# Eight views for the scattered results, and token tiles prepared only six places ahead, in a planned FFT and mixture-of-experts kernel

## The chip, the cores and the metric

The kernel runs on one core of one Trainium2 chip. The metric is the device time of one execution in microseconds (us). The engines carry the profile's names: PE (TensorE, matrix products), DVE (VectorE), ACT (ScalarE), POOL (GpSimd) and SP (SyncE, which here only starts DMAs).

## The reference

An input of 8 batches of 2496 rows by 256 columns goes through a real FFT along the rows, a complex 256x256 product with a bias, a soft threshold on real and imaginary part, and the inverse FFT. The 19968 rows that come out are tokens of a mixture of 8 experts, one expert for each token:

```python
Yr = Xr @ w_r - Xi @ w_i + b_r          # X = rfft(x, axis=1)
Yi = Xr @ w_i + Xi @ w_r + b_i
...                                      # soft threshold at 0.01
y = irfft(Y, n=2496)                     # 19968 tokens of 256
e_idx = argmax(y @ w_gate)               # one expert for each token
for e in range(8):
    h = maximum(y[mask] @ w1[e], 0.0)    # 256 -> 1024
    ye = h @ w2[e]                       # 1024 -> 256
    out[mask] = gate_w * eom * ye        # two factors for each token
```

Every product runs as three f16 products of values split into a high and a low half, so a matrix has two f16 parts.

## The kernel before, in words

The first part computes the FFT stages for one batch after another and writes the tokens `y`, with the two factors and the routing, to a DRAM tensor `yd`. The second part works on tiles of 128 tokens of one expert: T_A = 64 tiles in phase A, made of the tokens of batches 0 to 3 and taken in blocks of two tiles while the later batches still go through the FFT, and then 99 tiles in phase B, one to a block (tiles 64 to 162), made of the tokens of batches 4 to 7. Tiles of one expert follow one another, so the expert changes a few times in each phase.

A tile t takes these steps:

- `gathers`: an indirect DMA on POOL's queue fetches its 128 tokens into a place `yg` (6 places).
- `tokens`: DVE takes the largest magnitude of each token (`absmax` into `ym`) and makes a power of two from it (`pow2` gives `ys`, the scale, and its inverse, which goes into `fac` with the token's two factors). ACT writes the high f16 half of the scaled tokens to `yhl` (5 places), DVE the low half. A DMA with transpose, issued by SP, brings them to `eT`. There are three `eT` buffers, each for two tiles; in phase B a tile has one half of a buffer, and an even tile shares it with the next odd one. Its place is free when the up product of the tile six before is done.
- `up`: the product with `w1` in two halves, each of 4 groups of 128 hidden values. ACT evacuates the high half of the rectified result to `hh` and DVE the low half.
- `down`: the product of `hh` with `w2`. ACT scales the result by `fac` into `o` (5 places), and an indirect DMA on POOL's queue scatters its rows to `out`.

The weights of an expert are two halves of 1 MB (part 0 for up, part 1 for down) in three buffers `wbuf0` to `wbuf2`, which the blocks use by turns; `fetch` issues a load of each half for each block on SP, under a condition: only where the expert is another than that of the block three before. A new expert therefore loads its 2 MB into each of three blocks in a row. Part 0 waits for the up product of the block three before, part 1 for its down product.

The order on each engine is written by a planner (`Issue`, `io`): each step is a generator that yields either a condition ("up" of a tile, a free place) or an engine's letter (P, A, D, G, S for PE, ACT, DVE, POOL, SP) with a due time and a duration. The planner plays these and writes one fixed order for each engine, which the engines then follow with semaphores. In `tokens` the first condition is a free `yhl` place and a free number of `fac`; the two are also what limits how far ahead a tile is prepared. `small(1, "ym", bufs=3)` takes one of three small tiles by turns.

Names of matrix products in the profile: `ps<-eT,wbuf` (L1449) is up, `ps<-wbuf,hh` (L1415) is down. L1459 and L1460 are the evacuations of up, L1431 that of down, L1434 the scatter, L1324 the gather, L1343 and L1344 the two halves of `yhl`, L1310 a weight load, L1357 a transpose. In the changed kernel these lines stand 9 further down (L1324 and L1310: 3).

Of the kernel before, what the change touches and what calls it, by code (L numbers as in the profile page):

```python
# [11 lines left out]

# [1 line left out]
F32 = mybir.dt.float32  # L14
# [10 lines left out]
N = B * S  # L25
# [10 lines left out]
T_A = -((-(NA * S - E * 255)) // 256) * 2  # L36
# [110 lines left out]
EARLY = dict(yg=3, yhl=2, eT=1, hh=1, o=1)  # L147
PLACES = dict(yg=6, yhl=5, eT=3, hh=2, o=5)
UP, DN = 2.8, 1.4
KW = 4  # L150
YR, ZR, AN, WR, SR = 2, 3, 6, 3, 6
S1 = 6
# [35 lines left out]
class Issue:  # L188
# [64 lines left out]
    def give(self, slots, n=1):  # L253
        for _ in range(n):
            if slots.queue:
                self.go(slots.queue.pop(0))
            else:
                slots.n += 1
# [25 lines left out]
def tile_fft_moe(ctx, tc, x, w_r, w_i, b_r, b_i, w_gate, w_og, w1, w2, f1, f4, cmat, gmat, m16, out, dbg=None):  # L284
    nc = tc.nc
    V, A, G, T = nc.vector, nc.scalar, nc.gpsimd, nc.tensor

    pc = ctx.enter_context(tc.tile_pool(name="const", bufs=1, side="left"))
    psm = ctx.enter_context(tc.tile_pool(name="small", bufs=1, side="left"))
# [11 lines left out]
    def ring(pool, shape, dt, name, n):  # L301

        i = turn[name] = turn.get(name, -1) + 1
        return pool.tile(shape, dt, tag=f"{name}{i % n}", name=f"{name}{i % n}")

    def bank(i):
        return pps.tile([128, 512], F32, tag=f"ps{i}", name=f"ps{i}")

    def small(n, name, dt=F32, pool=psm, **kw):
        if "bufs" in kw or pool is psm:  # L310
            return ring(pool, [128, n], dt, name, kw.get("bufs", 2))
        return pool.tile([128, n], dt, tag=name, name=name)
# [71 lines left out]
    def absmax(m, src):  # L384
        V.tensor_reduce(m, src, AX.X, ALU.max, apply_absolute_value=True)

    def pow2(m, top, name, pool=psm, **kw):

        c = small(1, "p2c", bufs=3)
        V.tensor_scalar(c, m, 2.0 ** -40, 2.0 ** 60, ALU.max, ALU.min)  # L390
        e = small(1, "p2e", I32, bufs=3)
        V.tensor_scalar(e, c.bitcast(I32), 0x7F800000, None, ALU.bitwise_and)
        s = small(1, name, pool=pool, **kw)
        V.tensor_scalar(s.bitcast(I32), e, -1.0, float((254 + top) << 23), ALU.mult, ALU.add)
        inv = small(1, name + "i", pool=pool, **kw)
        V.tensor_scalar(inv.bitcast(I32), e, 1.0, float(-(top << 23)), ALU.mult, ALU.add)
        return s, inv
# [57 lines left out]
    def move(r, nbytes, issue, fn):  # L455

        yield "S", r, max(issue, nbytes / RATE), fn
# [602 lines left out]
    def plan(ph):  # L1060
# [30 lines left out]
        if ph == 0:  # L1091
            route["fl"] = pc.tile([1, T_ALL], I32, name="flg")
            route["ei"] = pc.tile([1, T_ALL], I32, name="ebi")
            V.memset(route["fl"][:, 0:2 * KW + 1], 1)
        V.tensor_copy(route["ei"][:, t0:t0 + n], ev[0:1])
        fl = lambda a, b, c, d, step: V.tensor_tensor(route["fl"][:, a:b], eb[0:1, a:b], eb[0:1, c:d:step], ALU.not_equal)
        if ph == 0:
            fl(4, 2 * KW, 0, 2 * KW - 4, 1)
            fl(2 * KW + 1, T_A, 2 * KW - 5, T_A - 6, 1)
        else:  # L1100
# [44 lines left out]
    sidx = pc.tile([128, T_ALL], I32, name="sidx")  # L1145
# [115 lines left out]


    W = []

    def open_w():
        yield "s1", B - 1
        yield "weights"
        s_x.close()
        pools["w"] = s_w.enter_context(tc.tile_pool(name="wexp", bufs=1, side="right", reuse_waits="tile"))
        for i in range(2):  # L1270
            W.append(pools["w"].tile([128, 8192], F16, name=f"wbuf{i}"))
        io.set("w open")

    def open_h():
# [3 lines left out]
        pools["h"] = s_h.enter_context(tc.tile_pool(name="hexp", bufs=1, side="left", reuse_waits="tile"))  # L1278
        W.append(pools["h"].tile([128, 8192], F16, name="wbuf2"))
        io.set("opened")  # L1280
# [4 lines left out]
    def place(k, i, shape, dt):  # L1285
        return pools["w" if i < EARLY[k] else "h"].tile(shape, dt, tag=f"{k}{i}", name=f"{k}{i}")

    def wplace(k):
        return k % 2 if k < KW else (k - KW + 2) % 3

    def before(k):

        return None if k < 2 or k == KW else k - 2 if k < KW else k - 3

    def fetch(r):

        yield "w open"
        for k, (t, n) in enumerate(BLOCKS):
            yield "plan", 0 if t < T_A else 1
            if k == KW:  # L1300
                yield "opened"
            for m in range(2):
                if before(k) is not None:
                    yield ("up", "down")[m], BLOCKS[before(k)][0]
                def f():
# [3 lines left out]
                    part = slice(4096 * m, 4096 * (m + 1))  # L1309
                    nc.sync.dma_start(W[wplace(k)][:, part], wd[ds(f, 1), :, part].rearrange("a p f -> (a p) f"), cond=g, cond_hint=False)  # L1310

# [4 lines left out]
    def gathers(r):  # L1316
        yield "w open"
        for t in range(T_ALL):
# [5 lines left out]
            yield "G", r + 5.6 * t - 30, 1.0, lambda: G.indirect_dma_start(out=yg, out_offset=None, in_=src, in_offset=bass.IndirectOffsetOnAxis(ap=gidx[:, t:t + 1], axis=0))  # L1324
            io.go(tokens(t, i, yg, r + 5.6 * t), io.now + 2.6)

    def tokens(t, iy, yg, r):

        il = yield slots["yhl"]
        yield slots["fac"]  # L1330
        m = small(1, "ym", bufs=3)
        fac = small(1, "fac", bufs=18)
        yhl = place("yhl", il, [128, 2, 256], F16)
        yield "D", r - 10, 0.41, lambda: absmax(m, yg[:, :256])

        def f():
            s, si = pow2(m, 2, "ys", bufs=3)
            V.scalar_tensor_tensor(fac, yg[:, 256:257], si, route["is"][:, t:t + 1], ALU.mult, ALU.mult)
            st["ys", t] = s

        yield "D", r - 10, 0.83, f
        s = st["ys", t]
        yield "A", r - 10, 0.5, lambda: A.activation(yhl[:, 0], yg[:, :256], AF.Copy, scale=s)  # L1343
        yield "D", r - 10, 0.48, lambda: V.scalar_tensor_tensor(yhl[:, 1], yg[:, :256], s, yhl[:, 0], ALU.mult, ALU.subtract)  # L1344
        io.put(slots["yg"], iy)
        if t >= T_A:
            ie = yield slots["eT1"]
            st["eT", t] = ie, part("eT", ie[0], [128, 2, 2, 2, 128])[:, ie[1]:ie[1] + 1]
        elif t % 2 == 0:
            ie = yield slots["eT"]  # L1350
            st["eT", t] = ie, part("eT", ie, [128, 2, 2, 2, 128])
            io.set("eT place", t)
        else:
            yield "eT place", t - 1
            st["eT", t] = st["eT", t - 1]
        eT = st["eT", t][1][:, t % 2 if t < T_A else 0]
        yield from move(r - 10, 1.4e5, 1.2, lambda: nc.sync.dma_start(eT.rearrange("p v c n -> p (v c) n"), yhl.rearrange("p v d -> p (v d)"), transpose=True))  # L1357
        st["fac", t] = fac
        yield TAIL
        io.put(slots["yhl"], il)  # L1360
        io.set("eT", t)
# [3 lines left out]
    def part(k, i, shape):  # L1365

        if (k, i) not in parts_:
            parts_[k, i] = place(k, i, shape, F16)
        return parts_[k, i]

    def back(k, t, i):

        if t >= T_A:
            io.put(slots[k + "1"], i)
            return
        st["n" + k] = st.get("n" + k, 0) + 1
        if st["n" + k] <= T_A // 2 - PLACES[k]:
            io.put(slots[k], i)
        else:
            for h in range(2):  # L1380
                io.put(slots[k + "1"], (i, h))

    def block(k, r):
# [12 lines left out]
        hh = hh.rearrange("p (v f n) -> p v f n", v=2, f=8)  # L1396
        w = W[wplace(k)][:, :4096].rearrange("p (c h v f) -> p c h v f", c=2, h=2, v=2)
        st["nu", t] = 0
        for half in range(2 * m):
            io.go(up(t, m, half, w, eT, ie, hh, r + UP * half * (m - 1)))  # L1400
        w = W[wplace(k)][:, 4096:].rearrange("p (i v c d) -> p i v c d", i=4, v=2, c=2)
        for i in range(m):
            io.go(down(t + i, m, i, w, hh, ih, r + (11.2 + 2 * UP * i + DN if m > 1 else 4)))

    def down(t, m, n, w, hh, ih, r):

        t0 = t - n
        yield "w", t0, 1

        def f(i=None):  # L1410
            if i is not None:
                st["pt", t] = i, bank(i)
            for fc in range(8 // m * half, 8 // m * (half + 1)):
                for k, (v, vw) in enumerate(((0, 0), (0, 1), (1, 0))):
                    T.matmul(st["pt", t][1][:, :256], hh[:, v, fc, 128 * n:128 * n + 128], w[:, fc // 2, vw, fc % 2], start=(fc == k == 0), stop=(fc == 7 and k == 2))  # L1415

        for half in range(m):
            for i in range(2 * half, 2 * half + 2):
                yield "hh", t0, i
            if half == 0:  # L1420
                yield "P", r, 2.62 / m, f, True
            else:
                yield "P", r + UP, 2.62 / m, f
        i, pt = st.pop(("pt", t))
        if n == m - 1:
            back("hh", t0, ih)
            io.set("down", t0)
        io_ = yield slots["o"]
        o = place("o", io_, [128, 256], F32)
        fac = st.pop(("fac", t))  # L1430
        yield "A", r - DN, 0.47, lambda: A.activation(o, pt[:, :256], AF.Copy, scale=fac)  # L1431
        io.free(i)
        give("fac")
        yield "G", r - DN, 1.0, lambda: G.indirect_dma_start(out=out, out_offset=bass.IndirectOffsetOnAxis(ap=sidx[:, t:t + 1], axis=0), in_=o, in_offset=None, bounds_check=N - 1, oob_is_err=False)  # L1434
        yield 3.6
        io.put(slots["o"], io_)

# [79 lines left out]
```

## Time and profile before

| what | value |
|---|---|
| runs | 1453.3, 1458.66, 1461.68 us (median 1458.66) |
| profiled execution | 1467.5 us, of which the span is 1465.7 |
| mean granted clock of PE | 0.991 |
| PE busy | 1410.3 us, 96% of the span |
| DVE, ACT, POOL busy | 975.2, 730.5, 646.1 us |
| phase B | about 930 to 1460 us of the span |
| HBM read and written | 337.44 and 58.91 MB |

A group of the profile names line, engine, operation and tiles (result <- operands, without buffer numbers). A time in square brackets behind an instruction is the idle time of its engine before it, with what ended it. The windows give for a stretch of the span each engine's busy time, the share of TensorE's full clock that was granted, and the busy share of the DMA engines.

### The profile page before, as it was taken

Reading aid. Unit: us, or ns where it says so; the run is one execution under the profiler, and the core shown is the slowest. Engines: PE = TensorE matmul, PEld = TensorE weight load, DVE = VectorE, ACT = ScalarE, POOL = GpSimd, SP = SyncE. Lnnn points to the kernel's source line nnn. Section 1 sums busy time; section 2 is a strip of 40 time slices with the busy share of each in tenths; the row PEclk is TensorE's granted clock in tenths of the full one; section 3 lists DMA queues with packets and bytes.
Section 4 is the critical chain, followed back from the end, with each engine's and each line's share of the span. In section 5 each row is a group of like instructions: output and inputs, shape, how many; then the busy total and the mean of one; then the engine's idle time right before and its main releaser. Section 6 shows DMA issues by size and latency. Waiting matters only on the chain.

```text
span 1465.7 us, 42645 instructions
## 1 busy us (share of the span) xinstructions
PE 1410.3 (96%) x16436; PEld 1276.6 (87%) x16436; DVE 975.2 (67%) x2789; ACT 730.5 (50%) x1413; POOL 646.1 (44%) x736
## 2 busy tenths in 40 slices
PE   5999999999999989999999999999998999999998
PEld 4998888898888868889988888899898989999898
DVE  4887767889998987787777855445454544554532
ACT  4777676868677664443333343333333333433432
POOL 2274565446575753355556343333333333433311
PEclk8999999999999999999999999999999999999999
DMA  7779899999997879976676679383846558387320
GB/s 199 174 170 212 204 233 203 229 226 224 221 218 190 180 246 178 282 210 217 192 213 209 189 234 266 100 241 92 225 125 185 166 151 237 83 239 215 97 49 24
DMA packets 294004, 276.47 MB, mean 189 GB/s; under 512 B 241846, under 2 KB 250168, under 8 KB 282025
## 3 DMA queue, kind: packets, MB, share of 16 engines
q1 hardware_dynamic: 277239, 229.68, 61.3%
q0 software_dynamic: 15872, 42.83, 10.6%
q8 instruction: 129, 2.11, 0.6%
q10 hardware_dynamic: 690, 1.24, 0.3%
q14 instruction: 74, 0.61, 0.1%
HBM read 337.44 MB, written 58.91 MB: 270 GB/s over the span
## 4 chain that ended last, share of the span: by engine, by line
PE 43%; DMA 10%; issue 4%; ACT 1%; DVE 1%; POOL 0%; POOLq 0%; SPq 0%; ACTq 0%
PE ps L1415 22%; PE ps L1449 21%; DMA eT<-yhl 4%; DMA out<-o,sidx 4%; DMA wbuf<-wd 2%; PE ps L1251 1%; ACT hh L1459 0%; DVE hh L1460 0%; ACT yhl L1343 0%; ACT o L1431 0%; DVE yhl L1344 0%; POOL out L1434 0%; POOL yg L1324 0%; POOL ob L1243 0%; POOLq L1513 0%
## 5 line engine op out<-in xcount | busy, mean ns | idle before, releaser
L1449 PE MATMUL ps<-eT,wbuf 128*128 128x128 f16 (+1 forms) x6288 | 462.4, 232 | 9.8 <-DMA wbuf<-wd 6.1
L1415 PE MATMUL ps<-wbuf,hh 128*128 128x256 f16 x3912 | 457.4, 273 | 9.2 <-ACT hh L1459 3.2
L1449 PEld LDWEIGHTS <-wbuf 128*128 128x128 f16 x6288 | 419.5, 98 | 32.6 <-DMA wbuf<-wd 7.4
L1415 PEld LDWEIGHTS <-hh 128*128 128x128 f16 x3912 | 378.4, 98 | 58.0 <-ACT hh L1459 5.1
L1460 DVE SCALAR_TENSOR_TENSOR hh<-ps,hh 128x512 f16<-128x512 f32 x326 | 219.6, 688 | 240.8 <-ACT hh L1459 215.2
L1434 POOL DMA_INDIRECT out<-o,sidx x163 | 163.2, 1001 | 427.1 <-ACT o L1431 214.6
L1459 ACT ACTIVATE hh<-ps 128x512 f16<-128x512 f32 x326 | 188.9, 596 | 270.9 <-PE ps L1449 235.0
L729 PE MATMUL ps<-whl,xt 128*128 128x256 f16 x1920 | 223.2, 273 | 0.9 <-ACT xt L714 0.7
L729 PEld LDWEIGHTS <-xt 128*128 128x128 f16 x1920 | 187.7, 98 | 32.6 <-issue 1.1
L1324 POOL DMA_INDIRECT yg<-yd,gidx x163 | 163.1, 1001 | 119.3 <-DVE yhl L1344 45.4
L1344 DVE SCALAR_TENSOR_TENSOR yhl<-yg,ys,yhl 128x256 f16<-128x256 f32 x163 | 79.0, 486 | 117.0 <-ACT yhl L1343 105.3
L1431 ACT ACTIVATE o<-ps,fac 128x256 f32<-128x256 f32 x163 | 76.9, 472 | 159.4 <-PE ps L1415 148.1
L1343 ACT ACTIVATE yhl<-yg,ys 128x256 f16<-128x256 f32 x163 | 81.9, 503 | 135.4 <-DMA eT<-yhl 83.2
L621 PEld LDWEIGHTS ps<-f1t,x 117*128 117x128 f32 (+1 forms) x704 | 88.4, 203 | 16.9 <-issue 14.6
L621 PE MATMUL ps<-f1t,x 117*128 117x120 f32 (+1 forms) x704 | 91.8, 288 | 0.2 <-ACT ste L776 0.2
L749 POOL TENSOR_TENSOR zhl<-z,zhl 128x512 f16<-128x512 f32 x54 | 62.8, 1163 | 51.0 <-ACT zhl L747 48.5
L1026 POOL TENSOR_TENSOR wsp<-wr,wsp 128x512 f16<-128x512 f32 x62 | 74.6, 1203 | 5.2
L759 PE MATMUL ps<-gt,zhl 128*128 128x128 f16 x960 | 65.5, 220 | 7.2 <-ACT zhl L747 3.0
L759 PEld LDWEIGHTS <-zhl 128*128 128x128 f16 x960 | 58.5, 98 | 14.1 <-ACT zhl L747 3.2
L825 PE MATMUL ps<-bdt,f4t 120*117 120x512 f16 x264 | 70.5, 382 | 0.1
L630 ACT ACTIVATE at<-ps,sx 128x480 f16<-128x480 f32 (+1 forms) x88 | 55.8, 650 | 28.8 <-PE ps L621 26.3
L631 DVE SCALAR_TENSOR_TENSOR at<-ps,sx,at 128x480 f16<-128x480 f32 (+1 forms) x88 | 59.2, 695 | 12.4 <-ACT at L630 12.1
(195 smaller groups left out, 1652.3 us busy)
## 6 DMA issues: line engine op xcount, KB each, us to landing
wbuf<-wd SPq DMA_DIRECT2D x262, 1024.0 KB
yd<-yt SPq DMA_DIRECT2D x120, 158.4 KB
x<-in_x SPq DMA_DIRECT2D x114, 156.0 KB
wr<-in_moe_w SPq DMA_DIRECT2D x32, 512.0 KB
wd<-wsp SPq DMA_DIRECT2D x64, 256.0 KB
yg<-yd,gidx POOLq DMA_INDIRECT x163
eT<-yhl SPq DMA_TRANSPOSE x163
out<-o,sidx POOLq DMA_INDIRECT x163
```

The costliest lines, as they stand in the source:

```text
L621: T.matmul(pv[:, dh, :, m * j:m * j + m], xs[:k, j0 + j, 128 * dh:128 * dh + 128], fw, start=True, stop=True)
L729: T.matmul(yp[:, 256 * j:256 * j + 256], xt_[:, v, 2 * dh + j, 64 - 64 * u:192 - 64 * u], whl[:, dh, vw, 256 * u:256 * u + 256], start=Fal ...
L759: T.matmul(bv[:, j], zhl[:, vz, c:c + 128], gt[:, 2 * p + j, v], start=(n == 0), stop=(n == 2))
L1324: yield "G", r + 5.6 * t - 30, 1.0, lambda: G.indirect_dma_start(out=yg, out_offset=None, in_=src, in_offset=bass.IndirectOffsetOnAxis(ap= ...
L1343: yield "A", r - 10, 0.5, lambda: A.activation(yhl[:, 0], yg[:, :256], AF.Copy, scale=s)
L1344: yield "D", r - 10, 0.48, lambda: V.scalar_tensor_tensor(yhl[:, 1], yg[:, :256], s, yhl[:, 0], ALU.mult, ALU.subtract)
L1415: T.matmul(st["pt", t][1][:, :256], hh[:, v, fc, 128 * n:128 * n + 128], w[:, fc // 2, vw, fc % 2], start=(fc == k == 0), stop=(fc == 7 an ...
L1431: yield "A", r - DN, 0.47, lambda: A.activation(o, pt[:, :256], AF.Copy, scale=fac)
L1434: yield "G", r - DN, 1.0, lambda: G.indirect_dma_start(out=out, out_offset=bass.IndirectOffsetOnAxis(ap=sidx[:, t:t + 1], axis=0), in_=o, ...
L1449: T.matmul(pt[:, 128 * m * j:128 * m * (j + 1)], w[:, dh, g // 4, vw, 128 * (g % 4):128 * (g % 4) + 128], eT[:, :m, v, dh], start=(n == 0) ...
L1459: yield "A", r, 0.6, lambda: A.activation(hv[:, 0], pt, AF.Relu)
L1460: yield "D", r, 0.69, lambda: V.scalar_tensor_tensor(hv[:, 1], pt, 0.0, hv[:, 0], ALU.max, ALU.subtract)
```

## The change

Three edits. The output tensor is seen through eight views that are tracked apart, and tile t scatters to view t mod 8; so a scatter no longer waits for the one before to land. `tokens` of tile t, from tile 6 on, waits until the up product of tile t−6 is planned (in phase A: of the block that holds it). The small results `ym` and `fac` are columns of two fixed tiles in place of rings of 3 and 18 tiles, and the ring of `ys` grows from 3 to 8.

```diff
+from concourse.ap import dram_disjoint_views
...
+AHEAD = 6
...
+    outs = dram_disjoint_views(out, 8)
...
+    facs = psm.tile([128, 18], F32, name="facs")
+    yms = psm.tile([128, 8], F32, name="yms")
+
     def tokens(t, iy, yg, r):
 
         il = yield slots["yhl"]
         yield slots["fac"]
-        m = small(1, "ym", bufs=3)
-        fac = small(1, "fac", bufs=18)
+        if t >= AHEAD:
+            p = t - AHEAD
+            yield "up", p - p % 2 if p < T_A else p
+        m = yms[:, t % 8:t % 8 + 1]
+        fac = facs[:, t % 18:t % 18 + 1]
         yhl = place("yhl", il, [128, 2, 256], F16)
         yield "D", r - 10, 0.41, lambda: absmax(m, yg[:, :256])
 
         def f():
-            s, si = pow2(m, 2, "ys", bufs=3)
+            s, si = pow2(m, 2, "ys", bufs=8)
...
-        yield "G", r - DN, 1.0, lambda: G.indirect_dma_start(out=out, ...)
+        yield "G", r - DN, 1.0, lambda: G.indirect_dma_start(out=outs[t % 8], ...)
```

The orders of the two kernels are equal until some 560 us into the span. From there on they differ on every engine; the numbers of instructions stay, but for seven multiplies of the FFT's output (`ob`) that move from POOL to DVE. On POOL, where a gather and a scatter alternate in phase B, a scatter before waits for the semaphore of the scatter before it, and now for that of the DMA eight places back on POOL's queue.

PE in the middle of phase B, before, one row of each group of matrix products (buffer and allocation number; `eT0`, `eT1`, `eT2` are the three buffers for two tiles each, an up product has two groups for its halves):

```order
L1449 MATMUL ps1_17460<-eT0_9673,wbuf0_9302 128x128
L1449 MATMUL ps4_17493<-eT0_9673,wbuf0_9302 128x128
L1449 MATMUL ps0_17522<-eT1_9773,wbuf1_9303 128x128
L1449 MATMUL ps2_17568<-eT1_9773,wbuf1_9303 128x128
L1415 MATMUL ps7_17596<-wbuf0_9302,hh1_9962 128x256
L1415 MATMUL ps3_17637<-wbuf1_9303,hh0_9917 128x256
L1449 MATMUL ps5_17704<-eT1_9773,wbuf2_9428 128x128
L1449 MATMUL ps6_17737<-eT1_9773,wbuf2_9428 128x128
L1449 MATMUL ps1_17766<-eT2_9825,wbuf0_9302 128x128
L1449 MATMUL ps4_17812<-eT2_9825,wbuf0_9302 128x128
```

PE at the same place after the change:

```order
L1458 MATMUL ps0_17343<-eT1_9763,wbuf1_9305 128x128
L1458 MATMUL ps7_17374<-eT1_9763,wbuf1_9305 128x128
L1458 MATMUL ps3_17401<-eT1_9763,wbuf2_9430 128x128
L1458 MATMUL ps5_17457<-eT1_9763,wbuf2_9430 128x128
L1424 MATMUL ps2_17486<-wbuf1_9305,hh0_9904 128x256
L1424 MATMUL ps1_17528<-wbuf2_9430,hh0_9904 128x256
L1458 MATMUL ps4_17583<-eT2_9815,wbuf0_9304 128x128
L1458 MATMUL ps6_17614<-eT2_9815,wbuf0_9304 128x128
L1458 MATMUL ps0_17641<-eT2_9815,wbuf1_9305 128x128
L1458 MATMUL ps7_17697<-eT2_9815,wbuf1_9305 128x128
```

Both run two up products and then two down products. Before, the two up products read different `eT` buffers, an odd tile and the next even one; now both read the same buffer, an even tile and the next odd one. The last pair before is (161, 162); now tile 162 stands alone at the end.

ACT in the middle of phase B, before (semaphores in brackets: PE, DVE and ACT's own, DMASW those of POOL's DMAs, DMAHW those of SP's):

```order
L1459 ACTIVATE hh0_9917<-ps2_19520 128x512 [waits PE_49,Activation_49]
L1431 ACTIVATE o4_19614<-ps7_19548,fac17_18174 128x256 [waits DMASW5_49,PE_49]
L1343 ACTIVATE yhl0_19578<-yg4_18922,ys1_19584 128x256 [waits DMAHW0_49,DMASW4_49,DVE_49]
L1343 ACTIVATE yhl1_19639<-yg5_18982,ys2_19649 128x256 [waits DMASW6_49,DMAHW1_49,DVE_49,Activation_49]
L1431 ACTIVATE o0_19682<-ps3_19589,fac0_18357 128x256 [waits DMASW7_49,PE_49]
L1459 ACTIVATE hh0_9917<-ps5_19656 128x512 [waits PE_49,Activation_49]
L1459 ACTIVATE hh0_9917<-ps6_19689 128x512 [waits PE_49,Activation_49]
L1459 ACTIVATE hh1_9962<-ps1_19718 128x512 [waits PE_49,Activation_49]
L1459 ACTIVATE hh1_9962<-ps4_19764 128x512 [waits PE_49,Activation_49]
```

and after:

```order
L1468 ACTIVATE hh1_9931<-ps4_19503 128x512 [waits PE_49,Activation_49]
L1468 ACTIVATE hh1_9931<-ps6_19534 128x512 [waits PE_49,Activation_49]
L1468 ACTIVATE hh1_9931<-ps0_19561 128x512 [waits PE_49,Activation_49]
L1352 ACTIVATE yhl3_19586<-yg2_18955,ys2_19612 128x256 [waits DMAHW2_49,DMASW4_49,DVE_49]
L1468 ACTIVATE hh1_9931<-ps7_19617 128x512 [waits PE_49,Activation_49]
L1440 ACTIVATE o2_19713<-ps3_19646,facs_146 128x256 [waits DMASW7_49,PE_49]
L1352 ACTIVATE yhl4_19671<-yg3_19020,ys3_19683 128x256 [waits DMAHW5_49,DMASW6_49,DVE_49]
L1440 ACTIVATE o3_19768<-ps5_19688,facs_146 128x256 [waits DMASW1_49,PE_49,Activation_49]
```

Before, the two preparations (`yhl`) stand together between the two results `o`, ahead of four evacuations of `hh`; now one stands ahead of the last evacuation and one between the results. The semaphore DMAHW that a `yhl` waits for is that of the transpose which last read its place.

SP in phase B, before:

```order
L1310 DMA wbuf1_9303<-wd_79 128x4096 [waits DMAHW2_49,PE_49]
L1310 DMA wbuf2_9428<-wd_79 128x4096 [waits DMAHW3_49,PE_49]
L1357 DMA_TRANSPOSE eT1_9773<-yhl2_25251 128x4x128 [waits DMAHW4_49,DVE_49]
L1357 DMA_TRANSPOSE eT2_9825<-yhl3_25434 128x4x128 [waits DMAHW5_49,DVE_49,PE_49]
L1310 DMA wbuf2_9428<-wd_79 128x4096 [waits DMAHW6_49,PE_49]
L1310 DMA wbuf0_9302<-wd_79 128x4096 [waits DMAHW7_49]
```

and after (the register loads between them are left out in both):

```order
L1313 DMA wbuf1_9305<-wd_79 128x4096 [waits DMAHW0_49,PE_49]
L1366 DMA_TRANSPOSE eT1_9763<-yhl1_25346 128x4x128 [waits DMAHW1_49,DVE_49]
L1313 DMA wbuf1_9305<-wd_79 128x4096 [waits DMAHW2_49,PE_49]
L1313 DMA wbuf2_9430<-wd_79 128x4096 [waits DMAHW3_49]
L1366 DMA_TRANSPOSE eT1_9763<-yhl2_25431 128x4x128 [waits DMAHW4_49,DVE_49]
L1313 DMA wbuf2_9430<-wd_79 128x4096 [waits DMAHW5_49,PE_49]
```

Before, two transposes stand together between the halves of every other block, the second waiting for an up product; now one transpose stands between the two halves of each block and waits for DVE alone.

More of the change, by code (lines that the diff above doesn't have):

```diff
@@ L1433, in down @@
         give("fac")
-        yield "G", r - DN, 1.0, lambda: G.indirect_dma_start(out=out, out_offset=bass.IndirectOffsetOnAxis(ap=sidx[:, t:t + 1], axis=0), in_=o, in_offset=None, bounds_check=N - 1, oob_is_err=False)
+        yield "G", r - DN, 1.0, lambda: G.indirect_dma_start(out=outs[t % 8], out_offset=bass.IndirectOffsetOnAxis(ap=sidx[:, t:t + 1], axis=0), in_=o, in_offset=None, bounds_check=N - 1, oob_is_err=False)
         yield 3.6
```

## Prediction

> **What bounds the kernel now.** I read the page first, then busy time by stretches of the span, then TensorE's list of waits, then the timeline around the longest of them. The page's head:
>
> ```profile
> span 1465.7 us, 42645 instructions
> PE 1410.3 (96%) x16436; PEld 1276.6 (87%) x16436; DVE 975.2 (67%) x2789; ACT 730.5 (50%) x1413; POOL 646.1 (44%) x736
> ```
>
> TensorE (PE) is idle for 1465.7 − 1410.3 = 55.4 us, and no other engine passes 67%. Whatever the change wins, it wins out of these 55.4 us. The stretches show where they lie (columns: us from the start, length, then busy us and instructions of PE, PEld, DVE, ACT and POOL, then PE's granted clock, DMA share and GB/s):
>
> ```profile
> 40.00:530.00 490.00, 484.62 (x5671) 430.15 (x5669) 414.23 (x1036) 359.84 (x691) 276.12 (x343) 1.00 0.89 208
> 550.00:900.00 350.00, 346.98 (x3260) 308.14 (x3257) 257.46 (x818) 137.43 (x269) 163.11 (x175) 1.00 0.77 218
> 900.00:930.00 30.00, 26.01 (x309) 23.41 (x307) 13.61 (x44) 9.34 (x19) 10.20 (x10) 0.96 0.74 197
> 930.00:1455.00 525.00, 510.00 (x6840) 477.03 (x6839) 253.91 (x785) 190.31 (x371) 174.77 (x176) 1.00 0.56 152
> ```
>
> The two orders are equal until shortly after 550 us, so of the idle time only 3.0 us (550 to 900), 4.0 (900 to 930, where phase A ends) and 15.0 (930 to 1455, phase B) are within reach, 22 us in all. What ended PE's waits from 900 us on (columns: waiting line, releaser, us in total, times, longest):
>
> ```profile
> PE ps L1449 <- DMA wbuf<-wd: 6.1, 7, 1.7
> PE ps L1415 <- ACT hh L1459: 3.2, 3, 1.8
> PE ps L1415 <- DMA wbuf<-wd: 2.8, 1, 2.8
> PE ps L1449 <- issue: 2.8, 8, 0.6
> PE ps L1415 <- DVE hh L1460: 2.0, 6, 0.3
> ```
>
> L1449 is the up product, L1415 the down product, `wbuf` the expert's weights, `hh` the hidden values. Weights come late, and ACT and DVE deliver `hh` late. Both happen at the expert switches. From the routing of these inputs the experts change in phase B at tiles 74, 86, 98, 110, 121, 133 and 142. At the seven places in time:
>
> ```profile
> 974.00:982.00 8.00, 6.97 (x104) 6.20 (x102) 3.91 (x11) 3.33 (x7) 1.98 (x2) 1.00 1.27 226
> 1041.00:1049.00 8.00, 6.43 (x94) 5.64 (x92) 3.94 (x11) 3.33 (x7) 1.98 (x2) 1.00 1.17 214
> 1109.00:1118.00 9.00, 5.21 (x74) 4.44 (x72) 3.81 (x11) 3.33 (x7) 1.98 (x2) 1.00 1.02 194
> 1177.00:1185.00 8.00, 6.68 (x101) 5.93 (x98) 3.67 (x11) 3.33 (x7) 1.98 (x2) 1.00 1.14 236
> 1236.00:1252.00 16.00, 15.47 (x202) 13.98 (x200) 9.67 (x31) 6.72 (x14) 5.51 (x6) 1.00 0.84 237
> 1297.00:1313.00 16.00, 16.00 (x233) 15.14 (x232) 6.96 (x25) 5.18 (x12) 4.96 (x5) 1.00 1.02 271
> 1353.00:1362.00 9.00, 6.08 (x85) 5.27 (x83) 4.23 (x12) 3.33 (x7) 2.93 (x3) 1.00 0.83 193
> ```
>
> Length minus PE's busy time gives 1.03, 1.57, 3.79 and 1.32 us at the first four, 0.53 and 0 at the next two, 2.92 at the last. The five that wait are those at even tiles (74, 86, 98, 110, 142), together 10.63 us. The two at odd tiles (121, 133) cost next to nothing. The reason is in the order: the up products run in twos, (odd, even), as two different `eT` buffers side by side show. A switch at tile s loads weights for the blocks s, s+1 and s+2. With s even, s+2 is the second of a pair, and its first weight half is wanted 2.7 us after the pair began; with s odd it is the first of a pair, and a pair of down products (5.4 us) stands ahead of it. The third switch (tile 98) in detail:
>
> ```profile
> 1105.63 5.02 SPq L1310 DMA_DIRECT2D wbuf<-wd  x4
> 1106.68 2.84 PE L1449 MATMUL ps<-eT,wbuf 128*128 128x128 f16 x48
> 1111.22 2.85 PE L1449 MATMUL ps<-eT,wbuf 128*128 128x128 f16 x48 [1.70 <-DMA wbuf<-wd]
> 1112.88 0.51 ACT L1343 ACTIVATE yhl<-yg,ys 128x256 f16<-128x256 f32 x1 [8.14 <-DMA eT<-yhl]
> 1115.84 0.39 PE L1415 MATMUL ps<-wbuf,hh 128*128 128x256 f16 x2 [1.76 <-ACT hh L1459]
> 1116.56 5.19 PE L1415 MATMUL ps<-wbuf,hh 128*128 128x256 f16 x46 [0.33 <-DVE hh L1460]
> 1111.93 0.99 POOL L1434 DMA_INDIRECT out<-o,sidx  x1 [7.16 <-DMA out<-o,sidx]
> ```
>
> 1.70 + 1.76 + 0.33 = 3.79, the whole idle time of that window. There are two chains. First the weights of the third block are late by 1.70. Then ACT, which runs in its written order, stands 8.14 us at the preparation of a tile far ahead (`yhl`, L1343), because its place is freed only when an old transpose has landed behind the weights; ACT's `hh` instructions are queued behind it, and the down product waits 2.09 for them. Over the kernel this wait of ACT, and the one of POOL in the last row above, are long:
>
> ```profile
> ACT yhl L1343 <- DMA eT<-yhl: 83.2, 25, 8.1
> POOL out L1434 <- DMA out<-o,sidx: 122.2, 51, 7.2
> ```
>
> **The change part by part.** *The scatters.* The eight views take away the 122.2 us in which POOL waits for the scatter before to land; the scatter then waits for the DMA of eight POOL transfers ago. On PE it is worth nothing that I can find: no wait of PE names `out`, `o` has five places, and ACT is not held by them. It could free ACT's evacuations a little at a switch (bound: no more than the 2.0 us under DVE `hh` above, most of which has another cause) or put more transfers onto a link that is already full:
>
> ```profile
> 1104.00:1108.00 4.00, 4.00 (x51) 3.71 (x49) 0.55 (x2) 0.47 (x1) 0.77 (x1) 1.00 1.02 402
> 1108.00:1112.00 4.00, 2.30 (x42) 2.13 (x40) 0.00 (x0) 0.00 (x0) 0.07 (x1) 1.00 1.45 132
> ```
>
> One 128x256 f32 scatter is 131 kB, 0.33 us at 402 GB/s, so an earlier scatter costs a weight load at most that much, and I count 0. [...]
>
> *The preparation, held back to six tiles.* Same instructions, later: it starts when the up product of tile t−6 is done and its place has then been free for long. ACT's order in phase B becomes hh hh hh yhl hh o yhl o, where it was o yhl yhl o hh hh hh hh. So the 8.14 us wait, and the 1.76 + 0.33 behind it, should go at every switch. The chain of one preparation is about 2 us on DVE and ACT, and the transpose must be there before up(t): five further tiles at 5.3 us (930 to 1455 holds 98.5 of them) are 26 us, against 13.4 us that the transpose at the switch above took from issue to landing (the longest I found). That lead covers it; without the cover (a preparation more than 12 us late) each switch would pay the difference on PE. SP's queue is where it can hurt: the transpose now waits for DVE, and the weight half behind it waits with it.
>
> ```profile
> SPq L1357 <- PE ps L1449: 80.0, 35, 5.6
> 1099.40 5.26 SPq L1357 DMA_TRANSPOSE eT<-yhl  x2
> ```
>
> Before, the same queue stood at the same transposes for the up product (80.0 us), since the transpose's `eT` place was bound to up(t−6) anyway. Now it stands there about 2 us longer, for DVE. The part-1 load behind waits for the down product of three tiles before, which ends later than that, so I count 0; bounds 0 and 2 us at each of seven switches, +14.
>
> *The pairs.* With the transposes single and in step with the up products, the planner's pairs become (even, odd): both products of a pair read one `eT` buffer, and tile 162 stands alone at the end. So the five even switches become the good kind. Their 10.63 us become 5 × 0.27 (mean of 0.53 and 0) = 1.3: −9.3. The two odd ones become the bad kind. Each pays the wait for weights, but not ACT's: the five switch waits of PE for `wbuf` at L1449 are 6.1 less 1.2 for two at the phase boundary = 4.9, or 0.97 each; 2 × 0.97 − 0.53 = +1.4. Bounds for the seven: −10.6 (no idle left) and 0 (each even switch as before).
>
> *The boundary of the phases.*
>
> ```profile
> 927.71 4.45 PE L1415 MATMUL ps<-wbuf,hh 128*128 128x256 f16 x24 [2.77 <-DMA wbuf<-wd]
> 928.00:930.00 2.00, 2.00 (x11) 1.44 (x10) 0.00 (x0) 0.00 (x0) 0.99 (x1) 0.50 0.00 0
> 930.00:932.00 2.00, 2.00 (x15) 1.52 (x14) 0.00 (x0) 0.00 (x0) 0.99 (x1) 0.67 0.33 93
> ```
>
> The down product of tile 66 waits 2.77 us for its weights. In the new order one more half of an up product stands ahead of it (24 matmuls, half of the 2.84 us of 48 above: 1.4), so −1.4 of the 2.77. After the wait the granted clock is 0.50 and then 0.67, which costs 2 × 0.50 + 2 × 0.33 = 1.7 us. Whether a shorter wait keeps the clock no row here shows: between 0 and −1.7 I take −0.8. [...]
>
> *Smaller terms.* The waits called issue (2.8 us, some 15 us after each even switch) I take to follow from the switch and halve: −1.4; bounds 0 and −2.8. Seven output multiplies of the FFT (`ob`) move from POOL to DVE, and
>
> ```profile
> PE ps L1251 <- POOL ob L1243: 2.1, 2, 1.5
> ```
>
> is what PE pays for them there: −0.5, between 0 and −2.1. At the end tile 162 has no partner whose product covers its `hh`: half 0 is evacuated in 0.60 on ACT (L1459) and 0.69 on DVE (L1460), 1.29 us plus hand-overs, against 1.4 of the other half, and then half 1 the same against 1.35 of down: +0.6. The last rows of the kernel
>
> ```profile
> 1461.30 0.47 ACT L1431 ACTIVATE o<-ps,fac 128x256 f32<-128x256 f32 x1 [2.19 <-PE ps L1415]
> 1462.26 0.97 POOL L1434 DMA_INDIRECT out<-o,sidx  x1 [1.91 <-ACT o L1431]
> ```
>
> leave 0.49 us between ACT's end and the scatter, of which a scatter free of its forerunner may save −0.1.
>
> Sum: −9.3 + 1.4 − 1.4 − 0.8 − 1.4 − 0.5 + 0.6 − 0.1 = −11.5 us. The profiled execution took 1467.5 us (1.8 around its span) and would take 1456.0. It lies 8.8 above the median of the runs, 1458.66; the same difference put on that gives **1447.2 us**.
>
> **The rivals.** *The waits only move.* Six megabytes must come through at each switch, at 402 GB/s 15.6 us whatever the pairing; if the late load now meets another product, or the runs without a profiler hold fewer of these stalls than the profiled one, only ACT's wait goes: the 3.2 + 2.0 us under `hh`, less tile 162's 0.6. About −4.6, 1454. For it: the share of 1.02; against: the two odd switches load the same 6 MB and lose 0.53 us together. *The larger gain.* All seven switches clean, issue and `ob` waits gone, boundary and clock recovered: −11.2 − 2.8 − 2.1 − 1.4 − 1.7 + 0.6 = −18.6, 1440. Against: the pairing leaves two switches bad. *Slower.* SP stands at a transpose for DVE, and weight loads queue behind it. It decides from the point at which the preparation ends later than the down product of three tiles before, some 5.3 us after up(t−6). Then each of seven switches gives back its gain and pays 2 to 3 us more: −11.5 + 9.3 + 7 × 2.5 − 1.4 = about +14, 1472. DVE is at 254 of 525 us in phase B, so a chain of 2 us rarely becomes one of 5: that speaks against. *The change does nothing it says.* The scatters keep waiting, or the order's pairing is undone by the chip; the order rules that out, since each engine follows its row.
>
> **How the numbers follow.** The forecast 0.52 (1443 to 1451), the larger gain 0.14, waits that only move 0.25, slower 0.09. About 0.5%, 7.3 us, is what a measurement of this kernel can tell from no change. Forecast and larger gain are faster, 0.65 with the edge of the forecast counted off; the moved waits are within 0.5%, 0.26 with that edge; slower 0.09. The range runs from 1440 (the larger gain) to 1459 (moved waits with the runs' own spread of some 4 us); above lies the slower case.
>
> **What would show it.** ACT's wait at `yhl` for `eT` (83.2) falls below 20 us and POOL's for `out` (122.2) to near 0. PE's idle time from 930 to 1455 falls from 15 to about 5 us, with what is left at tiles 121 and 133 (some 1240 and 1305 us) and under `wbuf`. The down product of tile 66 waits 1.4. PE waits under 1 us before tile 162's down product. I am wrong if SP's queue waits at L1366 for DVE and PE's wait for `wbuf` grows, if the even switches still wait, or if idle time appears in the FFT stretch, where the moved preparation meets DVE.

## The result: about half of the forecast gain

The changed kernel took 1448.48 us (median of 9 runs, 1444.29 to 1450.55) against 1454.46 for the kernel before in the same comparison (9 runs, 1450.11 to 1461.68): ratio 0.995, 95% interval 0.993 to 0.997. The forecast was 1447.2 within 1440 to 1459. The time fell into the range, but the gain against the runs beside it is 6.0 us and not 11.5. The profiled execution fell by more, from 1467.5 to 1450.28.

### The profile page after: what moved, and what is told of

Its sections match the earlier page's. It is cut to its first block, busy times and chain, and to the rows that moved or that the text cites. A ratio compares the mean times of both kernels' runs of the same rounds, so it can differ in the third digit from the quotient of the medians.

```text
span 1448.5 us, 42626 instructions
## 1 busy us (share of the span) xinstructions
PE 1402.4 (97%) x16436; PEld 1273.4 (88%) x16436; DVE 978.5 (68%) x2796; ACT 737.0 (51%) x1413; POOL 636.1 (44%) x729
## 4 chain that ended last, share of the span: by engine, by line
PE 45%; issue 29%; POOL 14%; DVE 6%; DMA 2%; ACT 2%; SPq 1%; POOLq 0%; ACTq 0%; DVEq 0%
PE ps L731 11%; PE ps L1458 9%; PE ps L1424 8%; POOL out L1443 7%; POOL yg L1327 7%; PE ps L623 5%; PE ps L761 3%; PE ps L827 3%; PE ps L701 3%; DMA x<-in_x 1%; PE ps L872 1%; PE ps L666 1%; PE ps L725 1%; PE ps L1253 1%; DVE z L747 1%
## 5 line engine op out<-in xcount | busy, mean ns | idle before, releaser
L1469 DVE SCALAR_TENSOR_TENSOR hh<-ps,hh 128x512 f16<-128x512 f32 x326 | 224.9, 690 | 275.8 <-ACT hh L1468 275.6
L1468 ACT ACTIVATE hh<-ps 128x512 f16<-128x512 f32 x326 | 194.6, 597 | 294.3 <-PE ps L1458 287.9
L1440 ACT ACTIVATE o<-ps,facs 128x256 f32<-128x256 f32 x163 | 77.2, 473 | 229.1 <-PE ps L1424 138.4
L1352 ACT ACTIVATE yhl<-yg,ys 128x256 f16<-128x256 f32 x163 | 81.7, 501 | 13.9 <-DVE ys L396 6.2
L633 DVE SCALAR_TENSOR_TENSOR at<-ps,sx,at 128x480 f16<-128x480 f32 (+1 forms) x88 | 59.3, 696 | 12.5 <-ACT at L632 12.3
```

The lines of the kernel that those rows point to most:

```text
L1468: yield "A", r, 0.6, lambda: A.activation(hv[:, 0], pt, AF.Relu)
L1469: yield "D", r, 0.69, lambda: V.scalar_tensor_tensor(hv[:, 1], pt, 0.0, hv[:, 0], ALU.max, ALU.subtract)
```

## The profile after

The head of the page of the changed kernel:

```profile
span 1448.5 us, 42626 instructions
PE 1402.4 (97%) x16436; PEld 1273.4 (88%) x16436; DVE 978.5 (68%) x2796; ACT 737.0 (51%) x1413; POOL 636.1 (44%) x729
```

PE's idle time is 1448.5 − 1402.4 = 46.1 us, 55.4 before. The stretches (columns as before: start and length, busy us and instructions of PE, PEld, DVE, ACT, POOL, then granted clock, DMA share, GB/s):

```profile
850.00:860.00 10.00, 7.28 (x52) 5.75 (x51) 3.00 (x10) 2.62 (x5) 3.06 (x4) 0.83 0.98 221
900.00:930.00 30.00, 28.71 (x356) 26.60 (x354) 15.28 (x49) 11.42 (x22) 11.22 (x12) 1.00 0.88 235
930.00:1440.00 510.00, 505.02 (x6831) 477.25 (x6830) 253.68 (x815) 193.40 (x374) 177.24 (x180) 1.00 0.58 157
```

Phase B's idle time is 5.0 us, 15.0 before, as forecast. PE's list of waits from 900 us on is now two lines, both for weights; every wait for `hh` and all called issue are gone:

```profile
PE ps L1458 <- DMA wbuf<-wd: 5.6, 5, 2.2
PE ps L1424 <- DMA wbuf<-wd: 0.6, 1, 0.6
```

The timeline shows where the larger ones are, tiles 123 and 135, the third blocks of the two odd switches:

```profile
1226.10 2.85 PE L1458 MATMUL ps<-eT,wbuf 128*128 128x128 f16 x48 [1.56 <-DMA wbuf<-wd]
1292.08 2.85 PE L1458 MATMUL ps<-eT,wbuf 128*128 128x128 f16 x48 [2.21 <-DMA wbuf<-wd]
```

One wait is new, in phase A. SP and PE around it (SPq is SP's queue; in the 6.12 us it issues three transposes and stands 0.6, 1.7 and 1.9 us at them for DVE; PE waits for the first of the three):

```profile
841.16 6.12 SPq L1366 DMA_TRANSPOSE eT<-yhl  x3
847.84 2.78 PE L1424 MATMUL ps<-wbuf,hh 128*128 128x256 f16 x24
853.34 4.16 PE L1458 MATMUL ps<-eT,wbuf 128*128 128x256 f16 x24 [2.72 <-DMA eT<-yhl]
```

That transpose, issued by 842.5 us, landed at 853.3, which is 2.72 us late for PE, and after the wait the clock fell: 24 matmuls took 4.16 us where 24 took 2.78 before it, and the granted clock from 850 to 860 is 0.83, worth 0.17 × 10 = 1.7 us. So the late transpose costs 4.4 us. The largest wait of SP's transposes in phase B is now this one:

```profile
SPq L1366 <- DVE p2e L394: 152.2, 40, 4.2
```

To compare phase B across kernels I use a number from the timeline: the time from one pair of up products to the next, summed over phase B, less 10.60 us for each pair, which is the period of nearly all undisturbed pairs. This excess was 21.5 us before and is 6.4 with the change.

## The experiments

All ratios are against the kernel before, run beside it, with the 95% interval in brackets. Odd pairs are (odd, even) as before the change, even pairs (even, odd) as after it; a switch is called even or odd by its first tile. The views alone leave the order of every engine as it was; the held-back preparation alone (with the new tiles) gives the changed kernel's order. So the change comes apart into three factors: the pairing, the holding back, the views. The new tiles for `ym` and `fac` were not run by themselves. The pairing can be set by itself, by rounding the due times of the blocks in phase B.

### Views alone (odd pairs, nothing held back)

```diff
+    outs = dram_disjoint_views(out, 8)
-        ... G.indirect_dma_start(out=out, ...)
+        ... G.indirect_dma_start(out=outs[t % 8], ...)
```

> Only the eight views of the output; every engine's order is that of the kernel before, the preparation is not held back. Theory (the order does it, the scatters nothing): within 2 us of before, about 1454; POOL's wait for the scatter before (122.2 us) is gone; PE still waits at the even switches, some 10 us together, and phase B's pairs of tiles still take some 20 us more than 10.60 each. Rival (the scatters' waits hold up ACT and so PE): most of the change's 6 us, about 1449.

Measured: 1456.53 against 1457.30, ratio 0.9995 (0.9969 to 1.0021). No gain. PE's waits from 900 us on:

```profile
PE ps L1417 <- ACT hh L1461: 7.3, 7, 2.0
PE ps L1417 <- DMA wbuf<-wd: 4.5, 1, 4.5
PE ps L1417 <- DVE hh L1462: 2.3, 7, 0.3
PE ps L1451 <- DMA wbuf<-wd: 2.3, 2, 1.6
```

POOL's wait for the scatter before is gone from the list, and PE still waits at all seven switches; excess 17.6 us. What the expectation did not see: the wait moved from weights to `hh`, and is now there at the odd switches too (1.97 and 1.94 us).

### Holding back alone (even pairs, six places, one view)

> Only the held-back preparation (with the fixed tiles for ym and fac), one view of the output; every engine's order is that of the changed kernel. Theory: the whole gain, ratio 0.995, about 1448.5; POOL's wait for the scatter before stays at over 100 us and PE's idle time in phase B is about 5 to 7 us, at tiles 121 and 133. Rival (scatters): about 1454, and PE waits for hh at switches because ACT waits for o.

Measured: 1457.36, ratio 0.9997 (0.9965 to 1.0029). Both theories were wrong. Phase B came out as the first had it, excess 4.6 us. The loss is in the FFT stretch, 550 to 900 us, where the changed kernel has 0.7 us in the same line:

```profile
PE ps L1253 <- POOL ob L1245: 11.2, 6, 4.6
```

The worst of the six, on POOL and PE:

```profile
739.52 1.01 POOL L1442 DMA_INDIRECT out<-o,sidx  x1 [1.21 <-DMA out<-o,sidx]
748.70 1.03 POOL L1442 DMA_INDIRECT out<-o,sidx  x1 [6.93 <-DVE ob L1224]
749.75 0.86 POOL L1245 TENSOR_TENSOR ob<-ob,t 117x396 f16<-117x396 f16 x1
750.67 0.49 PE L1253 MATMUL ps<-ob,ol 117*128 117x99 f16 x4 [4.62 <-POOL ob L1245]
```

The scatter at 748.70 stood 6.93 us. DVE's `ob`, which the line names, had ended at 747.95, after the scatter's own input was there (ACT at 743.85); the scatter issued at 739.52 began to report its landing at 747.25. An `ob` multiply is queued behind it, and PE waited 4.62 for that. In the changed kernel the same scatter went out at 741.47 and the multiply at 742.53. So with six places the views are needed: not for the MoE part, but so that a multiply of the FFT is not caught behind a scatter.

### The pairing alone (even pairs, nothing held back, one view)

```diff
-            io.go(block(k, r + 5.6 * t))
+            io.go(block(k, r + 5.6 * (t if t < T_A else t - t % 2)))
```

> The kernel before with up products paired (even, odd) in phase B by rounding their due times; nothing held back, one view. Theory A (the pairing decides where weights are late): PE's waits leave tiles 74, 86, 98, 110, 142 and appear at 121 and 133, where they are larger than 1.6 and 2.2 since ACT still waits for an old transpose and adds up to 2 us each; phase B's excess over 10.60 a pair falls from 21 to about 10 us, time about 1450 to 1452. Theory B (the held-back preparation does it, whatever the pairs): waits stay at all switches, about 1454.

Measured: 1450.13, ratio 0.995 (0.9924 to 0.9975), excess 6.6 us. Theory A holds, with less excess than the 10 us that it expected. This one line gives what the whole change gives. PE's waits from 900 us:

```profile
PE ps L1415 <- ACT hh L1459: 2.5, 2, 2.0
PE ps L1449 <- DMA wbuf<-wd: 2.1, 3, 1.2
PE ps L1415 <- DMA wbuf<-wd: 1.7, 1, 1.7
PE ps L1415 <- DVE hh L1460: 1.0, 3, 0.3
```

Of the even switches hardly anything is left; the third block of the switch at tile 133 waits 1.25 for weights and 2.01 + 0.33 for `hh`. Only 121 is smaller than expected, 0.20 + 0.47 + 0.33.

### The change with odd pairs

```diff
-            io.go(block(k, r + 5.6 * t))
+            io.go(block(k, r + 5.6 * (t if t < T_A else t - (t + 1) % 2)))
```

> The changed kernel with up products paired (odd, even) as before. Theory A: PE waits for weights at the five even switches, 0.5 to 2.2 us each, about 7 us together, without the waits for hh behind them; phase B's excess about 9 to 12 us (6.4 with the change, 21.5 before), time about 1451. Theory B (the held-back preparation alone does it): as the change, 1448.5, with waits at the odd ones no smaller.

Measured: 1465.27, ratio 1.006 (1.0034 to 1.0086): slower than before, which neither theory said. PE from 900 us, and SP in phase B:

```profile
PE ps L1458 <- DMA wbuf<-wd: 14.0, 5, 4.1
PE ps L1424 <- DMA wbuf<-wd: 5.7, 2, 5.6
SPq L1366 <- DVE p2e L394: 140.2, 36, 5.9
```

The waits are at the even switches, as theory A had it, but 14.0 us where I expected 7, and 5.6 at the boundary of the phases; four of the five switch waits are followed by matmuls at half rate (107 ns for 57). Holding back made weights later than they were here: SP stood at a transpose until DVE had prepared the tile (140.2 us in the 36 waits of the row above), and the weight loads queued behind went out late.

### The change with odd pairs, eight places ahead

Edit: that of the run before, and `AHEAD = 8`. Now the transpose waits again for the up product of the tile six before.

> The changed kernel with tiles prepared eight places ahead in place of six, and pairs (odd, even) as in the run of the change with odd pairs (1465.3 there, 1457.3 before). The transposes still wait for the up product six tiles before, so now the preparation is done when SP comes to them. Theory A (with six, SP stands at the transposes for DVE, 150 to 190 us in phase B, and the weight loads behind them go out late): that wait falls under 30 us, PE's waits for weights at the even switches fall from 14 us together to 5 to 8, time 1451 to 1456. Theory B (holding back itself or the views' scatters cost the time): stays at 1463 to 1466.

Measured: 1455.29, ratio 0.9995 (0.9973 to 1.0017). Theory A holds in the size: 0.65% came back. In phase B, SP's largest wait for DVE at the transposes, and PE's for weights:

```profile
SPq L1366 <- DVE facs L1347: 36.7, 35, 1.2
PE ps L1458 <- DMA wbuf<-wd: 3.0, 4, 1.8
PE ps L1424 <- DMA wbuf<-wd: 2.5, 2, 1.3
```

All of SP's waits for DVE there add to 49.5 us (192.3 with six), more than the 30 I expected. The wait for weights at the boundary of the phases, which lies before this window, has not gone: 5.66 us, 5.55 with six.

### The change, eight places ahead

> The changed kernel with eight places ahead in place of six; pairs stay (even, odd), views stay. Theory A: the waits at tiles 121 and 133 (1.56 and 2.21 with six) shrink to 0 to 1.3, the 2.7 us wait for a transpose in phase A (853 us) goes, time 2 to 5 us below the change: 1444 to 1447, ratio 0.992. Theory B (SP's order does not matter with these pairs): as the change, ratio 0.995.

Measured: 1444.27 against 1455.36, ratio 0.9928 (0.9901 to 0.9954); excess 4.8 us, and no wait for a transpose in phase A. The two odd switches cost 0.25 + 1.03 and 0 (1.56 and 2.21 with six), while the even one at tile 98 now costs 0.22 + 1.27. Theory A. The interval overlaps that of the change, so the step from six to eight is shown in the places that it names rather than by these two ratios.

### Even pairs and views, nothing held back

> The kernel before with pairs (even, odd) and the eight views; nothing held back. If the pairing is all of the gain, this is the ratio of the pairs alone, 0.995 (1450), with waits for hh of 1 to 2.5 us at tiles 121 and 133 because ACT still stands at yhl. If holding back is worth something that the pairs hide, the change is faster than this by 2 us or more.

Measured: 1459.97, ratio 1.0032 (1.0012 to 1.0052), where the pairs alone gave 0.995: the views cost 0.8% here. Not expected by either line. PE's waits from 900 us:

```profile
PE ps L1417 <- ACT hh L1461: 11.3, 8, 2.9
PE ps L1417 <- DVE hh L1462: 2.8, 9, 0.3
```

The orders of this kernel and of the pairs alone are the same, so only the waits differ. The DMA queues around the switch at tile 98 (a window that just holds all its loads; packets, MB, share of 16 engines), first with one view (1074 to 1100 us), then with eight (1080 to 1108); q1 is the hardware queue with the weights, q0 that of POOL's gathers and scatters:

```profile
q1 hardware_dynamic: 3187, 6.85, 86.5%
q0 software_dynamic: 295, 0.80, 8.9%
```

```profile
q1 hardware_dynamic: 2983, 6.80, 81.5%
q0 software_dynamic: 377, 0.94, 15.4%
```

The windows are 26 and 28 us long, so the weights take the same 22.5 and 22.8 us of the 16 engines, and POOL's transfers 4.3 in place of 2.3. With the views POOL sends 8 transfers in place of 7 while the weights come; from the first load's issue to the last one's landing it takes 25.2 us in place of 23.2, and the slowest transpose among them 12.9 in place of 9.3. At the five even switches these loads take 24.7 to 25.6 us in place of 22.6 to 23.3. So ACT stands 6 to 7 us at `yhl` at every even switch, where it stood 3.7 to 4.5, and its `hh` comes late. Its waits there in phase B, with one view and with eight:

```profile
ACT yhl L1343 <- DMA eT<-yhl: 57.6, 15, 7.9
```

```profile
ACT yhl L1345 <- DMA eT<-yhl: 68.4, 15, 7.0
```

They grow by 10.8 us, and PE's waits for `hh` by as much, from 3.5 to 14.1. In the changed kernel, whose 10 such transfers and 27.4 us are worse still, ACT has no wait at `yhl` for an old transpose, and PE does not notice.

### One up and one down product by turns, eight places ahead, views

```diff
-            io.go(down(t + i, m, i, w, hh, ih, r + (... if m > 1 else 4)))
+            io.go(down(t + i, m, i, w, hh, ih, r + (... if m > 1 else 8)))
```

> Eight places ahead and views, and the down product's due time 4 us later, so that one up and one down product alternate in phase B and no tile is the second of a pair. If the place in the pair decides, every switch has the same lead, 13.3 us between the load's release and its product against 10.7 and 16.0 in pairs: PE waits for weights 0 to 0.5 us at each switch, time 1440 to 1446. Rival: a lone up product does not cover the evacuation of hh (0.60 + 0.69 us and hand-overs, against 2.7 us), PE waits a little at each of 99 tiles, slower than the pairs.

Measured: 1461.58, ratio 1.0047 (1.0029 to 1.0065). My lead was worked out wrongly. PE in phase B:

```profile
PE ps L1458 <- DMA wbuf<-wd: 18.3, 9, 3.0
```

The rival is wrong as well: undisturbed tiles take 5.30 us, half of 10.60, so one product covers the evacuation. What counts, as far as the switch at tile 98 can show it, is not when the last load is released but when the first is, since all six come one after another (in the changed kernel they landed 5.6, 11.0, 13.9, 19.4, 21.9 and 27.4 us after the first issue). From the first load's issue to the moment when the third block's up product would run, it is 20.3 us with odd pairs and s even (1089.2 to 1109.5, before), 20.0 here (1078.6 to 1098.6), and 22.1 in even pairs (1076.5 to 1098.6, the pairs alone). The five megabytes up to that weight half landed 22.0, 22.9 and 20.6 us after the first issue. Two of the three are too late, and their waits are 1.70 and 2.88. Odd pairs do not fix this time: with the views alone it is 21.0 us (1078.9 to 1099.9), the half landed after 21.1, and PE's list has no wait for it.

### Eight places in phase B only, one view; six places in phase B only, views; eight places everywhere, one view

```diff
-        if t >= AHEAD:
+        if t >= T_A + AHEAD:
```

The three ran in one comparison, on an occasion on which the kernel before took 1465.53.

> Pairs (even, odd), preparation held back to eight places in phase B only, one view of the output; the FFT stretch and phase A have the order of the kernel before. Theory C (views hurt weight loads at a switch because POOL's transfers no longer wait: 22.6 to 23.3 us from the first load's issue to the last one's landing without views, 24.8 to 25.6 with; held-back preparation is only needed so that ACT does not wait for a late transpose): loads within 25 us, no wait of ACT over 4 us at yhl, PE's idle time at switches under 4 us together, time 1440 to 1445, ratio 0.990 to 0.993. Rival (views are needed to free o and yg): ACT's o or POOL's gathers hold up PE in phase B, 1448 or more.

> The change with the preparation held back (six places, views) in phase B only. If the change loses something in phase A and the FFT stretch (the 2.7 us wait for a transpose at 853 us), this is 2 to 4 us faster than the change: ratio 0.992 to 0.994. If not, 0.995 as the change.

> Eight places ahead everywhere, one view. With six and one view PE lost some 11 us in the FFT stretch to POOL (ob behind scatters that wait for the one before). If that comes from the scatters' chain, it is here again, ratio 0.998 to 1.001, against 0.993 with views; if it came from preparing at the last moment, it is gone, ratio 0.990 to 0.993.

Measured: 1451.54, ratio 0.9915 (0.9882 to 0.9949); 1456.22, ratio 0.9931 (0.9903 to 0.996); 1450.66, ratio 0.9904 (0.9871 to 0.9938). Theory C holds in the ratio, not in the time (1451.54, which is also what its rival named, but PE's waits at the switches add to 2.9 us and none is for `o` or a gather), and in ACT's waits but for one of 4.9 us before phase B. Its account of the loads does not hold: in the six switches whose loads are all in the trace they took 24 to 26 us (27.4 once) with one view, as long as with eight views and nothing held back. So long loads alone did not make PE wait here; ACT's stand at `yhl` behind them did, and in phase B it is 68.4 us there and 0 here. The views are not needed for any of this. Six places in phase B only gave the ratio of the first case, and no wait for a transpose in phase A, but its interval does not part it from the change; its profile also shows an excess of 16.3 us: 5.2 at tile 123, where PE waits 3.11 for weights and the clock falls (matmuls of 55 to 67 ns, then of 107), and the rest spread over nearly all pairs (10.6 to 11.2 us each), much of it in small gaps called issue, which I cannot explain. Eight places everywhere with one view have 0.2 us of waits for `ob` on POOL in the FFT stretch, though POOL's scatters there still wait 38.2 us for the one before. So the 11.2 us came from six places and one view together; why the scatters no longer catch an `ob` with eight was not tried further. This kernel, the change without its views and with 8 for 6, has the lowest ratio of all; from 0.9928 with views it is not parted, and the times themselves stand the other way round (1450.66, and 1444.27 with views on its occasion), so what the views are worth with eight places stays open.

### The kernel before once more

> The kernel before once more. Its first profile stood 8.8 us above the median of its runs. If the waits at the even switches belong to the order, they are here again at the same tiles with 8 to 15 us together; if the first profile was a bad draw in phase B, phase B's excess over 10.60 a pair is nearer 15 than 21.5 us.

Measured: 1470.94 (one run), excess 18.9 us, with waits at the same tiles, 12.5 us together (at 98 again the third-block wait of 1.85 plus 0.91 + 0.33). The order owns the waits. Their size varies: the excess is 21.5, 18.9 and, with views in the same order, 17.6 us, so the first profile was a somewhat bad draw in phase B.

## Why the forecast was right, and where it was not

*Even switches.* Forecast 10.63 to 1.3 us; the five now show 0.53 and 0.56 us at tiles 76 and 144 and no listed wait at the other three. Shown to be the pairing: pairs alone do it, and the change with odd pairs brings the waits back.

*Odd switches.* Forecast 0.97 each; measured 1.56 and 2.21. The term was too small because I costed SP's stand at the transposes at nothing. "The part-1 load behind waits for the down product of three tiles before, which ends later than that, so I count 0" is the step that failed: the loads behind the transposes did go out late. At tile 121 the fourth of the six loads went out 9.2 us after the first, and 7.9 with eight places; the fifth, for which PE waits, landed after 22.7 and 21.4. With odd pairs that alone turned the change into a loss (1.006, and 0.9995 with eight places). The slower rival named this mechanism, with seven places and 14 us; it was present at two, by my reading because only those had no lead to spare.

*ACT's wait at `yhl`.* Forecast to fall below 20 us; it is gone (83.2 before), and no wait for `hh` is left on PE. But the pairing alone leaves PE only 3.5 us of such waits, so with even pairs and one view there was little for the held-back preparation to win. With even pairs and eight views there was: 14.1 us of them and a ratio of 1.0032, where the change has 0.995. Inside the change, then, holding back makes good what the views cost at the switches, and the views what six places cost in the FFT stretch; the pairing is what is left as gain.

*The boundary.* The down product of tile 66 waits 0.59 for 2.77, and the clock stays at 1.00 from 928 to 932, where it was 0.50 and 0.67: the full 1.7 us, of which I had taken 0.8. This too goes with the pairing: the wait is 2.77 to 5.66 us in the five profiles with odd pairs and 0.33 to 1.92 in the eight with even pairs that have this boundary.

*Phase A.* Missed. "That lead covers it" was said of phase B's 26 us and not worked out for phase A's blocks of two. There the preparation of the tile that PE then waits for ended at 841.7 us, 11.6 before its transpose landed, and PE was ready 2.7 before that: 2.72 us, and 1.7 by the clock. SP's stand for DVE was 0.6 us of it; most was the way of the transpose, 10.8 us from its issue, with a weight load on the same queue from 840.7 to 850.3. Eight places, or six in phase B only, have no such wait.

*Tile 162.* +0.6 forecast, no wait seen: its up product ends at 1441.4 and the down product follows at once.

*The scatters.* Worth 0 by themselves, as forecast (0.9995). That an earlier scatter costs a weight load "at most" 0.33 us was wrong: with even pairs and nothing held back the views cost 0.8%, through late transposes (the slowest at tile 98 took 12.9 us in place of 9.3). At tile 98 POOL's transfers took 2.0 us more of the 16 engines (4.3 in place of 2.3), and the weights came 2.0 us later (25.2 in place of 23.2).

*The size.* Against its own profile the sum of −11.5 was too small: the profiled execution fell by 17.2. Part of that lies in how I added up waits. A wait is listed from the end that the profile gives for the matmul before it, and cost PE some 0.16 us more than its listed length (with a listed 0.33, 605 ns pass from one down matmul to the next in place of 109); phase B had 26 listed waits and has 4, by this estimate some 3.5 us. Against the runs the sum was too large, by nearly a factor of two: 6.0 us lies nearer to the −4.6 of the waits that only move, and it is the places of the waits, not the time, that tell the two apart. The step that failed is "the same difference put on" the median. The profile of before was 13.0 us above the median of the nine runs it was then compared with. Medians of the same kernel on four occasions were 1454.46, 1457.3, 1455.36 and 1465.53, so a single execution can carry a slow occasion. The waits in phase B are not all of it: the second profile of the same order took 3.4 us longer (1470.94) with 2.6 us less excess, and the profile with views in the same order took 10.2 us less with 3.9 us less. What else made the first one slow stays open.

## What to carry to other kernels

When two products are grouped, look at which member of the group a late load meets: here one line of due times that moved the pairs by one tile was worth as much as the whole change. A wait that is taken from one queue can go into another: here holding work back took ACT's 83.2 us at `yhl` away, and SP stood 152.2 us at the transposes for DVE, so hold it back only as far as the waiting engine needs (eight places and not six). Set a forecast difference against more than one profiled execution of the kernel before.

## What was not expected of the hardware

In these runs the length of a wait alone does not tell whether TensorE's clock falls. In the changed kernel it stayed at 1.00 around the wait of 2.21 us (1287 to 1297), and was 0.83 from 850 to 860, around the wait of 2.72. After a wait of 1.95 us (the change with odd pairs) the first three matmuls came at 56 to 66 ns and the next 32 at 99 to 108; after one of 2.71 us (products by turns) all 48 came at 55 to 66; after 2.57 and 3.11 us (odd pairs; six places in phase B only) the first 17 and 21 came at 55 to 67 and the following ones at 107, so there the drop showed only after the wait. In all traces, from 560 us on, the clock fell to 0.50 within 4 us of 15 of the 20 waits between 1.9 and 3.2 us, and of all seven longer ones (3.87 to 5.66).
